# A conformer block on one core: another table of block order and of PSUM banks

## The chip, the core and the metric

The kernel runs on one core of a Trainium2 chip. The core has five engines that run their own instruction streams and meet through semaphores: TensorE (PE), whose weight loads (PEld) run beside its matmuls, VectorE (DVE), ScalarE (ACT), GpSimd (POOL) and SyncE (SP), which here issues the DMAs. PE writes its results to PSUM, of which the kernel uses banks 0 to 7; the other engines read them from there and keep everything else in SBUF. The metric is the device time of one execution in microseconds (us), as a median of several runs.

## The reference

One block of a speech model, for 2 sequences of 4000 tokens with 144 channels, in bf16: a feed-forward layer, self-attention with 4 heads of 36 channels, a gated convolution of 5 taps, another feed-forward layer, a last layernorm. The helpers (layernorm, softmax, silu, sigmoid) are the usual ones.

```python
def reference(x, w_ff1a, w_ff1b, w_qkv, w_o, w_pw1, dw, w_pw2, w_ff2a, w_ff2b):
    B, T, D = x.shape
    K = dw.shape[0]
    H = 4
    Dh = D // H
    h = _layernorm(x, axis=-1)
    h = _silu(h @ w_ff1a) @ w_ff1b
    x = x + 0.5 * h
    h = _layernorm(x, axis=-1)
    qkv = h @ w_qkv
    q = (lambda x, *d: x.transpose(*d))(qkv[..., :D].reshape(B, T, H, Dh), 0, 2, 1, 3)
    k = (lambda x, *d: x.transpose(*d))(qkv[..., D:2 * D].reshape(B, T, H, Dh), 0, 2, 1, 3)
    v = (lambda x, *d: x.transpose(*d))(qkv[..., 2 * D:].reshape(B, T, H, Dh), 0, 2, 1, 3)
    scale = Dh ** (-0.5)
    scores = jnp.einsum('bhqd,bhkd->bhqk', q, k) * scale
    p = _softmax(scores, axis=-1)
    att = jnp.einsum('bhqk,bhkd->bhqd', p, v)
    att = (lambda x, *d: x.transpose(*d))(att, 0, 2, 1, 3).reshape(B, T, D)
    x = x + att @ w_o
    h = _layernorm(x, axis=-1)
    h = h @ w_pw1
    a, b = (h[..., :D].copy(), h[..., D:].copy())
    h = a * _sigmoid(b)
    pad = K // 2
    hp = jnp.pad(h, ((0, 0), (pad, pad), (0, 0)))
    c = jnp.zeros_like(h)
    for i in range(K):
        c = c + hp[:, i:i + T, :] * dw[i][None, None, :]
    x = x + _silu(c) @ w_pw2
    h = _layernorm(x, axis=-1)
    h = _silu(h @ w_ff2a) @ w_ff2b
    x = x + 0.5 * h
    return _layernorm(x, axis=-1)
```

The costly part is the softmax attention: for each sequence and head there are 4000 x 4000 scores, 128 million in all, and each needs an exponential.

## The kernel before

**Tiles.** The 8000 tokens are 16 chunks (`CH` = 500), 8 for each sequence. Attention runs over chunks of queries; for each it walks the keys in tiles of 64 rows. One key tile and one chunk make a *tile of scores*: 64 keys by 500 queries for 4 heads, computed by a *quartet* of four 64x64 matmuls (`PS<-QT,KT`), each into half the partitions of one of two neighbouring PSUM banks. The exponential of a tile is a single ACT instruction over both banks, 128x1000 (`PT<-PS`), or, for some of the tiles, a few DVE instructions that build the exponential from the bits of a number (int16, then two uint16 operations and a product, also `PT<-PS` and `PT<-PT`). The result lies in one of 11 buffers of `PT`. A quartet of four matmuls of 64x37 (`PS<-PT,VA`, "PV" below) then sums values and weights into the two banks 6 and 7, which hold the output of the chunk until all its key tiles are through.

**Background.** Everything else goes on between these tiles: layernorms (`ST`, `RS`, `XN`, `AN`: statistics on DVE, the scaled rows on POOL or DVE), DMAs that turn rows into columns through a scratch tensor (`rows`, `XT`, `XTQ`), projections (`WQKV`, `WQ`), feed-forward tiles (`PS<-XT,WA` and `PS<-XT,WE`, then `TH`, a tanh on ACT, and `HT`, a product on DVE), residuals (`PS<-WB,HT` for a feed-forward layer, `PS<-WO,XT` after attention, `PS<-WP,SW` after the convolution; DVE adds them to `X`), the gate and the convolution (`PS<-XT,WP`, `U`, `PS<-U,DG`, `SW`), and small fillers on PE (`PS<-IDENT`). The front of the run is feed-forward and projections of the first sequence, until there are keys to attend to; the tail is the last chunk's convolution, second feed-forward layer and layernorm.

**How the order comes about.** The program is written as generators, one for each piece of background work, and a loop that plays the engines' clocks forward in a cost model. `Rec.op` records every operation with its dependencies, and each step of that loop makes one *block*: the operations of one step on one engine, such as the four matmuls of a quartet. On PE there are 2866 blocks, on ACT 1094, on DVE 1663, on POOL and SP some hundred each. When all 15,425 operations are recorded, `Rec.reorder` (line 263) puts the blocks of every engine into another order, read from the table `ORDER`: the character at place i of an engine's string says by how many places block i is moved (line 270):

```python
shift = [ALPHABET.index(c) - 45 for c in table[e]]
...
    at[i + shift[i]] = blk
```

`P` leaves a block at its place, `Q` moves it one place later, `O` one earlier. A second table, `PLACES`, gives one digit for each PSUM tile in the order in which tiles are taken: the first of its banks, 0 to 5 (`Rec.place`, line 241). After the move, `Rec.reorder` works out again which PSUM tile follows which in a bank, in the new order of PE, so that the first matmul of a tile waits for those that read the tile before it; it also sets which PV matmul of a sum starts it and which ends it. `Rec.finish` (line 323) turns the dependencies into semaphore waits, and `Rec.replay` (line 367) sends each engine its line of operations. Each engine runs its line strictly in order, so a waiting instruction holds up all behind it. All instructions are recorded under line 377, which is in `replay`; they are told apart by engine and tile names. The end of the kernel is

```python
R.reorder(ORDER)
R.finish(group_qs=("w0", "w1", "w2", "w3"))
```

Of the kernel before, what the change touches and what calls it, by code (L numbers as in the profile page):

```python
# [39 lines left out]
        "VOOROOBPPQOUPQMPRUQRTLQTQDPIPPQQQQQUQQHMRVOLRNNNPPPTOOOOPPPPQOROQRVOVPQMNPTROWQSLOUNOPXOUROMVMNZOS-R"  # L40
        "MKMOOOQOPQXQOLOOOOOXOOOPNOOOXOOOPNQNTMTOMNXNPNP_OLNQOLRNNN]OMRMOUKVMNYQMRPQHTYCMOLOWOMNNOROQLQOPTOOO"
        "ORROQLPVOOOOOUNOPPQQKPPPPPPPROSPRLTMTNNNOROOUORNORLORPQQSKO[_PYQRNOIFINLTLNNQNPSSNTMMYQNRRSMMSNUOCUP"
        "NYOVPROOJORRTNS>NNPTTOMNNUOOORNNTOOOOXROQSPPSQGXPPPPVOOOTROUSPPUQGPP3PPPQOPPPQRNOSOPXPPQOPVPQRPKBWSO"
        "OQNJOPZPNRNNNQQ]MQOQHPMSPPMKPPPPP^UOOPKMQRLQLRLNVPXMNNQMMTNNROMQQNURNOWRPMIQNNPPRRSNPKPPPPQQNPPPPPUP"
        "PPPQYIOOOOTNNOMRPRRVSPLXNSSMNTUOTJNTRMR8MPQSSOLQQTKQNNSPVMQMNOQNTQSMRNRJOUOOPNOQTNPSSLYLMRRMM]PNQIPM"
        "ORTMSOKQJSSSOSVJRPHPKPQOQOUPNOOQNPQRNOPPSOPNSOSQSQKRPRSOFRRMRMOSQSMRRKMRPNRUSMOTKMPTM_TRLMNQOPRSQMMW"
        "TOOOORO:VPNOOOOPQOPQOQOPROOPPPVOPQOWKPUOKOOVQOIOOOPPPPSOSOPRUQQHLXPPPQOVP_FLNNTMPNWZMPMGLMUMPNLOPQOP"
        "QOPQQURTNJOTROINSOOOQOTOOOQXMOOOPXMNNOOOOOPROOPPQOPPPPPPPPQOPPPPQSPUWQWIKPWJPJQVPQRKSNRfNPPQSSMNNb8R"
        "MMMRLMSMNQSLUN_ZOKNPN>TOLLMRLNQOSQOMPROURPNWO_HNNNNPPLOYNPRRKKPKSPMRN`RMQMMRSMMQNVVNVPXLNPRR@NSVO[NO"
        "OSNOVPMPNPTROSQSZROSQT(EOTJMOSQSNSJNSSPLULOO]NPMWNOOPKMNVMOOSNUMTLNNSMOTXMNNNOPNO]PNOTQNLMNOOORTQMMO"  # L50
        "PQRPSPPQUSGPTQQWQQUQTNCCMRPYPLOOSOOLRMOPPQ]QMNQOWOKNOMNRPRVJNRPMMQOURTMNLNSPSQLWROURPVZQTQTRW?ERAQGQ"
# [2019 lines left out]
```

## Time and profile before

| What | us |
|---|---|
| median of three runs | 887.04 |
| lowest and highest of them | 886.72, 887.05 |
| the profiled execution, a further one | 887.44 |
| its span, first to last instruction | 885.6 |
| wide exponentials on ACT, 128x1000 (806) | 749.1 busy, 1.075 each |
| feed-forward and gate activations on ACT (TH, 198) | 105.1 busy |
| scores on PE (3968 matmuls) | 425.6 busy |
| PV on PE (4712 matmuls) | 410.8 busy |

The granted clock of TensorE has a mean of 0.999 in the profiled execution, so the throttle plays no part. "Busy" is the time in which an engine had at least one instruction under way; a group's time is that of its own instructions. In the form `out<-in` the profile names the tiles that an instruction writes and reads with the buffers' numbers left out, and `[0.16 <-DVE HT L377]` behind an instruction says that the engine was idle for 0.16 us ahead of it and that the end of the wait came with DVE's write of `HT`. Lists of instructions in order of time give the start, the time from there to the end of the last of the group, and how many there were in a row. Matmuls of one row overlap: two quartets one behind the other start 0.21 us apart, though each is listed with 0.38.

DMA is idle for the most part (13.7% of 16 engines' span in the queue that carries nearly all of it), and POOL is busy for 303.9 us, a third of the span.

### The profile page before, as it was taken

The page shows a single profiled execution, that of the slowest core. Times are in us where ns is not written, and L with a number is a line of the kernel's source. Part 1 is how long each engine was busy: PE and PEld are TensorE (multiplying, and loading weights), DVE is VectorE, ACT ScalarE, POOL GpSimd, SP SyncE. Part 2 cuts the span into 40 slices and gives each one's busy share as a digit, 9 for nine tenths or more (in the row PEclk, how much of TensorE's full clock was granted, in tenths as well). Part 3 has the DMA queues.
Part 4 walks back from the last instruction along what each step waited for, and adds up shares of the span by engine and source line. Part 5 has one row for each costly group of instructions (what it writes and reads, how often), then busy time and mean ns, then how long its engine had stood idle before and what let it go on. Part 6 is the DMA issues. An engine that isn't in the chain of part 4 may idle for free.

```text
span 885.6 us, 27130 instructions
## 1 busy us (share of the span) xinstructions
PE 857.2 (97%) x11478; PEld 385.1 (43%) x11478; DVE 818.4 (92%) x1799; ACT 851.5 (96%) x1095; POOL 303.9 (34%) x584
## 2 busy tenths in 40 slices
PE   8999999999999999999999999999999999999996
PEld 7544333444444434344344444443434343444466
DVE  7968999999999999999988899997988999999987
ACT  6799999999999999999999999999999999999974
POOL 7761500216235235024107125241631017022733
PEclk9999999999999999999999999999999999999999
DMA  4231011112211111212101111002011001101101
GB/s 101 45 61 36 23 37 31 34 23 44 44 30 23 37 30 27 47 24 43 23 19 28 30 32 29 22 17 51 22 37 24 7 15 45 29 9 36 37 17 34
DMA packets 114222, 28.81 MB, mean 33 GB/s; under 512 B 101085, under 2 KB 114100, under 8 KB 114100
## 3 DMA queue, kind: packets, MB, share of 16 engines
q1 hardware_dynamic: 112642, 26.46, 13.7%
q8 instruction: 90, 1.47, 0.7%
q10 hardware_dynamic: 1458, 0.62, 0.3%
q14 instruction: 32, 0.26, 0.1%
HBM read 13.44 MB, written 13.61 MB: 31 GB/s over the span
## 4 chain that ended last, share of the span: by engine, by line
ACT 43%; PE 39%; DVE 14%; POOL 1%; DMA 1%; SPq 1%; issue 1%; DVEq 0%; POOLq 0%
ACT PT L377 39%; PE PS L377 39%; DVE PT L377 8%; ACT TH L377 4%; DVE ST L377 1%; DVE HT L377 1%; DVE X L377 1%; POOL XN L377 1%; DVE QT L377 1%; DVE XN L377 1%; DVE KT L377 1%; SPq L377 1%; DMA XTQ<-rows 1%; POOL RS L377 0%; DVE VA L377 0%
## 5 line engine op out<-in xcount | busy, mean ns | idle before, releaser
L377 ACT ACTIVATE PT<-PS 128x1000 bf16<-128x1000 f32 (+1 forms) x822 | 756.3, 1066 | 5.0 <-PE PS L377 3.8
L377 PE MATMUL PS<-QT,KT 64*64 64x500 bf16 x3968 | 425.6, 385 | 14.0 <-ACT PT L377 8.3
L377 PE MATMUL PS<-PT,VA 64*37 64x500 bf16 x4712 | 410.8, 372 | 2.0 <-DVE PT L377 0.7
L377 DVE TENSOR_SCALAR PT<-PS 128x500 int16<-128x500 f32 x372 | 244.6, 669 | 8.0 <-PE PS L377 6.5
L377 PEld LDWEIGHTS PS<-QT,KT 64*64 64x64 bf16 x3968 | 124.5, 104 | 240.3 <-ACT PT L377 135.5
L377 POOL TENSOR_SCALAR RS<-ST 125x4 f32<-125x4 f32 x130 | 35.2, 271 | 459.9 <-DVE ST L377 453.7
L377 PEld LDWEIGHTS PS<-PT,VA 64*37 64x37 bf16 x4712 | 141.2, 96 | 96.4 <-DVE PT L377 20.7
L377 POOL TENSOR_SCALAR XN<-X,RS 125x144 bf16<-125x144 bf16 x260 | 153.0, 622 | 8.0 <-DMA out_dram<-XN 1.3
L377 DVE TENSOR_SCALAR PT<-PT 128x1000 uint16<-128x1000 uint16 x372 | 150.6, 416 | 1.9 <-PE PS L377 0.5
L377 DVE TENSOR_TENSOR PT<-PT 128x1000 bf16<-128x1000 bf16 x186 | 126.5, 682 | 1.4
L377 ACT ACTIVATE TH<-PS 128x500 bf16<-128x500 f32 (+3 forms) x198 | 105.1, 554 | 4.0 <-PE PS L377 2.7
L377 POOL TENSOR_TENSOR RS<-RS,NHALF 125x4 f32<-125x4 f32 (+1 forms) x93 | 91.5, 987 | 36.2 <-DVE RS L377 30.4
L377 DVE SCALAR_TENSOR_TENSOR HT<-TH,PS 128x500 bf16<-128x500 bf16 (+1 forms) x135 | 80.8, 617 | 17.7 <-ACT TH L377 16.9
L377 PE MATMUL PS<-XT,WA 128*128 128x500 bf16 (+4 forms) x288 | 74.9, 365 | 0.4 <-DVE AN L377 0.2
L377 DVE BATCH_NORM_STATS2 ST<-X 125x6 f32<-125x288 bf16 x160 | 65.6, 446 | 3.1 <-DMA X<-in_x_dram 2.9
L377 DVE SCALAR_TENSOR_TENSOR X<-PS,X 125x288 bf16<-125x288 f32 (+1 forms) x128 | 57.2, 451 | 9.7 <-PE PS L377 8.6
L377 PE MATMUL PS<-WB,HT 128*125 128x144 bf16 (+1 forms) x640 | 51.9, 230 | 0.6 <-ACT HT L377 0.4
L377 PEld LDWEIGHTS PS<-WB,HT 128*125 128x125 bf16 (+1 forms) x640 | 44.2, 136 | 14.0 <-issue 4.6
L377 POOL COPY U<-U 128x2 bf16<-128x2 bf16 (+1 forms) x54 | 12.0, 260 | 71.4 <-DVE U L377 71.4
L377 PEld LDWEIGHTS PS<-XT,WA 128*128 128x128 bf16 (+1 forms) x288 | 21.2, 97 | 34.0 <-issue 12.5
L377 PE MATMUL PS<-U,DG 128*128 128x375 bf16 (+6 forms) x204 | 29.0, 264 | 0.2 <-DVE PT L377 0.2
L377 DVE STREAM_TRANSPOSE XN<-XN 128x320 f32<-128x320 f32 x54 | 27.0, 500 | 1.7 <-POOL XN L377 1.6
(93 smaller groups left out, 533.3 us busy)
## 6 DMA issues: line engine op xcount, KB each, us to landing
rows<-XN SPq DMA_DIRECT2D x216, 40.0 KB, 2.0
XT<-rows SPq DMA_DIRECT2D x56, 128.0 KB, 2.0
rows<-AN SPq DMA_DIRECT2D x60, 40.0 KB, 2.0
X<-in_x_dram SPq DMA_DIRECT2D x16, 140.6 KB
XTQ<-rows SPq DMA_DIRECT2D x26, 70.3 KB
out_dram<-XN SPq DMA_DIRECT2D x13, 140.6 KB
XT<-rows SPq DMA_DIRECT2D x56, 16.0 KB, 1.9
out_dram<-XN SPq DMA_DIRECT2D x3, 70.3 KB
```

What stands on the lines that cost most here:

```text
L377: ins = getattr(eng, o.name)(*o.a, **o.k)
```

## The change

Only the two tables change: five strings in `ORDER` and the digits of `PLACES`. In the strings, 1706 of PE's 2866 characters are different, 92 of ACT's 1094, 780 of DVE's 1663, 71 of POOL's 129 and 23 of SP's 154; 166 of 1720 digits in `PLACES`. The operations, their shapes, the buffers in SBUF and the code that reads the tables stay. With the new strings an operation may stand earlier or later on its own engine, a PSUM tile may lie in other banks, and the waits between the engines follow from that.

```diff
 ORDER = {
     "pe": (
-        "PPPPPPPPQOPPPRRRNLPPQSPROQQQHTOPPMRPRMQNV[NZMMMtMKPMOLIOOOQNQORRNTYLVESPPKLRPEEOOOQNPP[PNQNNQOMPP^PP"
-        "JPNPNQ[TLNKMQOKPNSQMNUOOOROSPPQXRGNPROUQYHKNNPNPNQQMPPPQOPWXNNNNPMM]]MNNOMQNLQLMMPPPTOOOOPPPQOUOOOOO"
-        "TWQWQKLJQNRPWITNNVOLLOORNOQOSYNNPMZNNNOMOOVN[PMSJPLQKQSQWQXHRWRVQRYWRHXR=BRALJRTMVOLWTLMPMPUUHOWORLO"
...
+        "PPPPPPPPQOPPPRRRNLPPSSOOLQQQMTOOPNQOPQQN|^N^MNNrJLNNNNHHLLMOOLQOQTWJVGRTNGHQSFFHMMOOPP]PNPNOQOMPPPQQ"
+        "JQOQOROVSOLNROLQQSPLOUOOOROSPPQXRGNYROUQIJKNNPUPNOPNPPPROOPVOOOOPNPUPNOOQNQOTQOPLPPPPPPPPPPPPPPPPPPP"
+        "TPQWQKPQQNRPFSUNOUOKPMOQ[NQNRXLMPL^LMMNRNNSMZOLTKOPNJPRPVPWIQVQUPQXVQQWQBCQ@KWQTLPYKTULINLOWTJOXORLN"
...
     ),
     "act": (
-        "PPPPPPPPPPPPQRSMNOPRPQQQKPPQOPQOPUOOOOOPPPRPQSQUNIVSSNORIIPPPPPPPPPPPPPQOPPQOPPPPPPPPQOPPPPPPPPPPPPP"
...
+        "PPPPPPPPPPPPQSSMNNSQNNQQNPPQOPQOPXOOOOOOOOPQQNSUOMTVTKLSKLMPPPPPPPPPPPPQOPPQOPPPPPPPPQOPPPPPPPPPPPPP"
...
     ),
     "dve": (
-        "PPQOQQQMPPQOaOOOOQR`MNJNOPLRNNYYHPMKOPJRNQJQQNRROQQQQIUPUPNSSSTGSSSTFSFRSSURUICZJSLOLPVOPNIXNNORNNPM"
...
+        "PPQOQQQMPPRPbMOOOQR`MNJNOPLQNNYYHOOLOPHRNQJQQNRROQQQQISSTOQ`RbSGGOPRIQIQSPRRUGEVTVEMKQVQRIIXMNORNNPM"
...
     ),
     "pool": (
-        "PQQQQSSOORPQTQOPQQTQQNQQQQQRRORPQQQQQ,PXOOOOOOO_NORNSMMNNOOQNNPWSNNOMPQQQKTTNNNNQQNPPPROTPMTOPTKNROQ"
...
+        "PQQQQRSOPRPQTQOPQQSQSNPQQQQQQSQOQQQQQ,PPPPPPPPPUOOOO]NROMNOVNNOMRMMPXOOPPMPPQQKUSNXMNLOOTNQSLPRJQRPQ"
...
     ),
     "sp": (
-        "PPPPPPPPQOPPPPPPPPPPPROQSMRNNPPPPPPPPPPPQOQOPPPPWOVNNNNNNPPPPPPRRNNRRNNPPPPPPPPRRNNPPZOOXNOMNNNNNVOO"
...
+        "PPPPPPPPQOPPPPPPPPPPPROQRMQNPPPPPPPPPPPPSOOQNPPPWOVNNNNNNPPPPPPRRNNRRNNPPPPPPPPRRNNPPZOOXNOMNNNNNSOO"
...
     ),
 }
 PLACES = (
-    "5024031421242530124140023035304230343105232504015043214352103245041522040241204124012401314032034023"
-    "2403240240340242043024034024032023403520430243024303420242034203402540524025405240524052404250524052"
...
+    "2341304015523150434105323035304230244135413412203025315242502403101510340241204124012401314032034023"
+    "2403240240340342042034024024032032404220430243024303420242034203402540524025405240524052404250524052"
...
 )
```

More of the change, by code (lines that the diff above doesn't have):

```diff
@@ L42 @@
[L42 to L51, printed above, removed]
@@ new lines @@
+        "OZPWQRHQKPLRWOS<OOPWJPNOOOOPPSOPNPPPPPSPPQQQQQHPQRRRRMQQQQQRTQNVRPQQ<QQHRPQQQKSOPTPQKQQSPPWQRSQLCUSJ"
+        "ORNKPQYQOLOPPMRRM[PQJQMTMPMMQQQQJZVOOPKMQULQKRLNWPXMNNPMMPNXQOMQOMYRNOPVINPMMVPPPPTOHOOPPPPPPPPPPWPP"
+        "PPPPYHOOOOTNNOMRPSQVTPLXNSSLNTUOTJNTRMR8MPQRYSLSQNLSHNVQLNQNNPRORNTNSPSTPVPRGGPRLORTTMYLNRSJN]KOQKPM"
+        "RNTMSOKVKUNTNSWLQQJFOOPPPPPSOOOQOPQVNPPPWOQOQOTRTRLSQSTPHSSNSNPRR3NSSPNSQOSVRNEULNQMN_SSNLMQOPRSQMMW"
+        "WOOOQOM=TPNOOQOPQOPXOOOPNOOOPPVOOOOPNPUOQOPVQOIOOOPPPPSOOOPRUQRMKYPPPPIPP[OKOOXNPNXZMMMGMNUMPNKOPUOO"
@@ new lines @@
+        "QOMSQTNXPJSPNOIO[OOOQNNOOOPXMOOOQOMOQOPPPQRNOPPPPPPRPNPPPQQNPPPPPTPY[QTJKP[IQJRLQQTKOORfOROQURLOMb6R"
+        "LMMRLNSMNQVLSNOYTKORN=TPKMRRMNROSNPNRRNUMPNVO[LNNNNPQMNWNVPQKNOJRPNROdRMQMMTTMNNNVQNVPVMNPTR?NSVOYNO"
+        "ORNOVPQQLPSXORPSYPNRPS(ENSMRNSPRORIORROSUKNNTNPMWNOOPSMNVMOOSNOMYSNNOMOPWMNUNOMNN_PNOOQNQMNOOOOSQMNP"
+        "PPPPVOPPSPKTUQOVPQUPROBERZOTPKOOKOOQQMPPRO^QMNRPSMKNRMNRPRVJNQQMMQOVTOMOMNSPSQLWROURPVZQTQTRS?ERAQGQ"
+        "QQ_PPPPPRFQRMKPPLYWNNPMOLNRROYSOZNFOLOXNOXNNGNNNOOeQNROOPUOPNWQMMBOMNSMPMRPNURNNSQNUPIQUMPLSOP]PJUNO"
@@ new lines @@
+        "MRNUKOOJQNPPYOORNNPQOWJOOOOPNSOOOPPPQOPPPPSPNUROOPQQTGOROTXKOMNPNRNNRXOMOPNOPNSTNN_MP_LNOQLYPKORIMMO"
+        "QUEOPPMQOPPTOPNURROMUPROOQSPTUQOLWOQ:NOOOPPPPPPPZTOP[QLPHTOPHKNOZOOOPNOOSORNKQOPPQQQZLOOOOOQOPLXOOOQ"
+        "NNOXNQNNOOPQWLOOOOOTNOOVNOOOOOTOOOTNOVNWPNWOPHWPISKPNWPZHQXNQVJQKFRRKQRWOEOPNPNPRORNOPWOQOQOPRROUFOO"
+        "OOP]OOOOOOOOOUOQNPQQQGP]OOOOOOQZNOSJMRLOLQRMRROLPPPSQUNPKSQTLPSOROSVOS_TN^[QNGIQOLLNNNW^1NNNNNPQOWJO"
+        "OLOPNPPQOPPZOORPNVOOINNRNOPVOPNQNTRLNVMOOOOO]OOOOOOOOOQNNPQ]NOOQRM]SKTVQITQWGGGROIdMOPQOLcVNLOPROSHJ"
@@ new lines @@
+        "NN[DNOMQMQOKOZRMVPLLNPNLPQOPPPUXOMYNLOLOMOOOPPPPQOSTPM[OKOO_NPQOSJNQHPQORRH[LOOOPNO[NNZMMNNXMOMN]IMN"
+        "NOOOOOWOMWMNYMMMQMMVOMNOOOUPNOOOPROOPPVOOXNOOLOOOOPXSOOQNPIOWOOOQNNOUSPURKKLUNOWPNLOOPQMQQNQRNOUQNPM"
+        "QQQLSQUSQSUMWPFFTOOKSVPNRXXNFKQWLLLMQUMRLNRPSSJNUROSJMNRTNVRcMTINRSNSFNOZFOOLOORWJZLLPULPKLOTLXUMMQL"
+        "MULTMNUMQUNOIORNOPPRRVNLOQORVKPMYPMPPRPVTGWJLMVLNNNPUMQOMTNPNOZOOORNNNOOOPPPPPPPPPTPSMOTPQJSPPKROOPS"
+        "OOOPPPPPPPPPQQRSQRRIVSSPSSKUCYQGRMQJYOOJXNNNNNNRNRMOPWOQZPMVNPPGPJQLPTROMNPPTPPPQTPXOGNOOOOQNPTRPMRP"
@@ new lines @@
+        "PPPQOPPPPPPPPPPPPPPPPPPPPPPPPPPPPPPPPPPPPPPPPPPPPPPPPPPPQOPPPPPPPPPPPPROORORNOQOPPPPPPPPPPPPPPPPPQOP"
+        "QQNPPQOPPPPPPPPPPPPPPPPPPPPPPPPPPQOPPQOPPPPPPPPPPPPROOPPPPPPPPPPPPPPPPPPQOPPPPPPPPPPPPPPPPPPPPPPPPPP"
+        "PQOQOPPPPPPPPQOPPPPPPPPPPPPPPPPPPPPPPQOPPPPPPPPPPPPPPPPPROQNPQQNPPPPPPPPPPPPPQOPPPPPPPPQOPPPPPPPPPPP"
+        "PPPPPPPPPPPPPPPPPSOOOPPPPPPPPPQOPPPPPPPPPPPPPPPPPPPQQNPPPPQOPPPPQQNPPQOPPQOPQOQOPPPPQOPPPPPPPPPPPPPP"
+        "PPPPPPPPPPQOPPPPPPPPPPPPPPPPPPPPPPPPPPQOPPROOPPPPPQOPPPPPPPPPPQOPPPPPPPPPPPPPPPPPPPPPPPPPPPPPQOPPPPP"
@@ new lines @@
+        "QOQOPPQOPPPQOPPPPPPPPPPPPPPPPPPPPPPPPPPPPPPPQQNPPPPPQOPPPPPPPPPPPPPPPPPPPPPPPPPPPPPPPPPPPPPPPPPPPPPP"
+        "PPPPPPPPPPPPPPPPPPPPPQOPPPPPPPPPQOPPPPPPPPQOQOQOPPPPPPPPPPPPPPPPPPPPPPPPPPPPPPPPPPPPQQQMPPPPPPPPPPPQ"
+        "OQOQOPPPPPPPPPPPPPPPPPPPPPPPPPPPPPPPPPPPPPPPPPPPPPPPPPPPPPPPPPQOPPPPPPPPPPQOPPPPPPPPPPPPPPPQOPPPQOPP"
+        "PPPPPPPPPPPQOPQOPPPQOPPPPPPPPPPPPPPPPPPPPPPPPPPPPQOPQOPPPPPPQOPPPPPPPPPPPPPPPPPPPPPPPPPPPPPPPPPPPPPP"
+        "PPPPPPPPPPPPPPPPQQNPPPPPPQOQOPPPPPPPROOQOQOPPPPQOPPQQQMPPPPROOSQNNQQQMRRSSPKKPPPPPPPQQQQLPPRPN"
@@ new lines @@
+        "PPQOPPQOROOQOQOQOPQOPcPNOOOOPQOQKNOOOOPNQORRSMVLNPNOOPPPPQSVPSQJRRIQSQSTPUUWPSG?JLOPPPPPUPUPPQSIPQSP"
+        "PQWQOQOPP=QOQOPROOSOSOPRKOPPPQQ_PLOOQNPPLO]NOOLOOPNOOSQMQLQOQOTRORNQJYOQOPPKPPMPPPQOPPTOTOOLOQQQQQSS"
+        "OSSPLRPBRPNPPPPPPPPPPQQRPQQQSHROQQQQQVQOEOTOMOQQSQRNQQRRORSBRMQXQRNRRMRURRORHRROQ;QQQRSOJSPRSQJQQQTP"
+        "SOOURBNNSNORNOROOQOPQOROOROOPPQOQOTPNPQUPKQNQMPPPSPNSPMOQSNOZQMQRNOQOPGPPPPQOPPPPPPXPNOOOPNOQOQOQQTQ"
+        "TPURTJPEQQIROOUQOQOQTPTOORDNQOQOPQQNQSPSLNOPPPPPPPQTPQRKRTQJSOROQQQQQSQSQMRPQSPUOP7P`PPPPPPPPPPCOOOO"
@@ new lines @@
+        "PRPNQOQOQOPPPPPPQOPPPPPPSOOSNOORORNRNQNPROOQOPPPPgOPNOOOPNOOOOOOQNNOOSNNNPPPPPPPPPQOROOPQOPRRNRPQKPP"
+        "PPROOPRPNQRNOQQNPQOQQNROOPPQOQRNQRMQNQQNQQNPPPQOPPPPPPPQQNPROOPQOQOPQUPPUOOPPQSQDNSOOOPPPPPSQORPRPRP"
+        "RPSDOQNPPQRPSPPQIQQNPPPPPPRRNNQQNQOPPQOPPPPPPQOPPPPPPPPPPPPPPPPRORPTLPUMUPLMNOPQQNPPQOPQOQOQOPPPPPPP"
+        "PPQQQQQKPSOOOQOPQOPQOPPTPPMOPPPROORPVPLOOOOPPPPPPPPPPQOPPRPNmPNOOOWNNNNNNNNOPNOPNPNQQMQORPIPQQRMRNOP"
+        "PPPPQOPPPPPPPPPPQOQOPQOQOPPPPPQOPPPPPPPPPPPPPPPPPPPPPPPSOPNPPPPPPPPPPPPSOOOPPPPQOPPPQQNRTNSMRMSLOOPQ"
@@ L98 @@
+        "OPQOYPRPRPJQRIQLPPPQOPPPPPPQOQOPRPNRPRPRPQIPSOORNOPQOQOSPN_ROLNQNUPLOLNPMSOOOQOPSSNSNLOPQOPPPPPQOPPP"
+        "QOPQOPPPPPPPPPQQQRPQQVPPPEOOPPPPPPQOQOPPPQTQSNKNPPPQRNOPQTQMRSLTOTJORLQQQKPSPRMNPPPQOPPPPPPPPPPPRSNP"
+        "RPKPPQQNPPPPPPROOSOOOPROOPPQRPQRROTQQSMROBPPPPROSNPSPPTRSSMRRKCRPQMPROQNPQOQOPPPSTOMPQRKOQOPQQQQRbQI"
+        "QOKOabQMMMNPNROTQQS@EGQQUPTQTCTW[NR^TTKCKBKLPPPKORSTNQXQQHPPQOF"
     ),
     "pool": (
-        "PQQQQSSOORPQTQOPQQTQQNQQQQQRRORPQQQQQ,PXOOOOOOO_NORNSMMNNOOQNNPWSNNOMPQQQKTTNNNNQQNPPPROTPMTOPTKNROQ"
@@ L106 @@
+        "OPZOOXNNNNNNNNTZNNNNOOOOVNNZNNNNOOOOOTNOPNPPPPPPPPPPQO"
     ),
@@ new lines @@
+    "3024203430243024024013402140204124024012042140204254052042502540425042504250542204303401340134013402"
+    "1402140234015310530153015302034204202430243203420342034302425042504240214205342034034014302430243024"
+    "3024032430243024302440254025402502052504524024023502352052405240524041204012412420140214021402140214"
+    "0214021402140214102141204021421431043103402141034204034014302535103502450425034204302403420342034203"
+    "5302430243024302430242040214034203413402045240524120425042540524052042021402014201421402140204240204"
@@ L127 @@
+    "1204120412041204102402424120412041214120401240214021402041204204523055203205240524052350235024302430"
+    "2430243034203420342034304024203240324024203350350230242420054311042401340242043203420420240124505240"
+    "2530523502325040254120423052350533203420423045240240250301542605436113451104506531532463145652501641"
+    "31401302321460502536"
 )
```

72 lines of the change are left out of this document (14 added, 58 removed).

## The prediction

> **What bounds the kernel now.** First the busy times, the chain of waits and the costliest groups on the page, then a table of busy time by stretch of the span.
>
> ```profile
> span 885.6 us, 27130 instructions
> PE 857.2 (97%) x11478; PEld 385.1 (43%) x11478; DVE 818.4 (92%) x1799; ACT 851.5 (96%) x1095; POOL 303.9 (34%) x584
> ACT 43%; PE 39%; DVE 14%; POOL 1%; DMA 1%; SPq 1%; issue 1%; DVEq 0%; POOLq 0%
> L377 ACT ACTIVATE PT<-PS 128x1000 bf16<-128x1000 f32 (+1 forms) x822 | 756.3, 1066 | 5.0 <-PE PS L377 3.8
> ```
> ```profile
> 0.00:40.00 40.00, 36.89 (x400) 25.77 (x401) 33.32 (x107) 28.53 (x56) 30.21 (x74) 1.00 0.34 79
> 40.00:80.00 40.00, 39.05 (x537) 17.35 (x537) 29.89 (x69) 38.56 (x53) 19.17 (x37) 1.00 0.23 52
> 80.00:800.00 720.00, 704.46 (x9554) 295.79 (x9555) 677.40 (x1417) 716.47 (x879) 217.82 (x410) 1.00 0.13 29
> 800.00:840.00 40.00, 38.97 (x542) 16.92 (x534) 39.78 (x88) 39.49 (x49) 20.39 (x38) 1.00 0.16 35
> 840.00:886.00 46.00, 37.81 (x466) 29.26 (x464) 38.02 (x122) 28.45 (x62) 16.34 (x28) 0.98 0.10 26
> ```
> The columns are PE, PE's weight loads, DVE, ACT and POOL. From 80 to 840 ACT is busy 716.47 + 39.49 = 755.96 of 760 us, idle 4.04, and the chain goes to and fro between ACT's exponentials and the matmuls that feed them. PE's 97% says less: its weight loads waited 148.4 us for ACT's PT in the table of waits, so PE is often full only because it is held up.
>
> Idle time hides part of ACT's waiting, because one activation can begin before the one ahead of it is done:
> ```profile
> 399.57 9.12 ACT L377 ACTIVATE PT<-PS 128x1000 bf16<-128x1000 f32 x10
> ```
> Ten in 9.12 us, of a shape whose mean is 1.07: less one for the last, nine spacings in 8.05, 0.89 each. Over the trace the 806 wide exponentials begin after each other by 0.884 in the shortest half, 0.900 at three quarters and 0.964 at nine tenths. What every ACT instruction takes beyond the fastest tenth of its own shape is waiting: 8.4 us in 0–40, 2.6 in 40–80, 21.1 in 80–840, 12.9 after that. No order can win more than this 45.0 from ACT's side. Of the middle's 21.1, 13.9 lie in 99 waits in which PE was still busy with other blocks when it should have begun the producer, 2.9 in gaps under 0.03, and some 4.3 in waits where PE itself waited for DVE or ACT.
>
> **The change part by part.** Every operation stays, with its shape: nothing is removed or added, so busy time keeps its sum, and only waits can change. Moved to another place on their engine are 7012 of PE's 11,478 instructions, 861 of DVE's 1799, 356 of POOL's 580, 57 of SP's 465 and 92 of ACT's 1103. So ACT runs nearly its old sequence, fed in another order. Changes between 64-square and full-array matmuls on PE go from 782 to 776, and waits on semaphores change by at most 10 on any engine (PE 1956 to 1963, DVE 1409 to 1419): I take both at nothing. The 57 moves on SP are loads and stores of background rows; the chain gives DMA and SP's queue 1% each, and ACT's middle waits name none of them: nothing.
>
> *Front (0–80).* PE sets it:
> ```profile
> 27.93 0.39 PE L377 MATMUL PS<-PT,VA 64*37 64x500 bf16 x4
> 28.25 0.63 PE L377 MATMUL PS<-XT,WA 128*128 128x500 bf16 x2
> 29.04 2.71 PE L377 MATMUL PS<-WB,HT 128*125 128x144 bf16 x40 [0.16 <-DVE HT L377]
> 31.68 0.41 PE L377 MATMUL PS<-QT,KT 64*64 64x500 bf16 x4
> ```
> ACT waits 2.64 us there for the scores that begin at 31.68, behind the 40 residual matmuls. In the new order one more feed-forward tile stands ahead of the residuals and the scores come later still, but the same ACT operations and almost the same PE work stand ahead of the exponential that begins at 44.70. What leaves the stretch ahead of its scores (44.16) is one PV quartet with its two changes of array form (27.93 to 28.25 = 0.32) and 4 of the 32 small projection matmuls (4/32 of about 0.64 = 0.08): −0.40. The bound above: the tile moved ahead of its operand stalls for one DVE HT (0.59) and one residual (0.68) is not hidden: +1.3. I take −0.40, because the work ahead is counted and the stall is not seen.
>
> *Tail (840–886).* PE sets it from 838 to 874 apart from a table load at 855:
> ```profile
> 858.78 0.84 PE L377 MATMUL PS<-WB,HT 128*125 128x144 bf16 x10 [0.25 <-ACT HT L377]
> 859.45 0.23 PE L377 MATMUL PS<-WP,SW 128*125 128x144 bf16 x1
> 859.52 0.23 PE L377 MATMUL PS<-WP2Z,SW 80*125 80x144 bf16 x1
> ```
> The four conv-projection matmuls from 859.45 (0.26) now stand ahead of the residual at 858.78 and fill its wait of 0.25: −0.25. In DVE's order two layernorm statistics (0.73 to 0.85 both) come ahead of the last chunk's, so its normalised rows come 0.65 later; that costs nothing while PE has its fillers and residuals from 860 to 870, and 0.35 to 0.65 if not. The other end, −0.75, is two more such waits filled. The last stretch from the final residual at 873.75 has the same order on DVE. I take −0.25.
>
> *Middle (80–840).* For each ACT instruction I took how its producer moved on PE against the ACT instruction ahead, weighing each matmul passed by its pace in the trace (a quartet of scores or PV 0.21, a feed-forward tile 0.44 to 0.46, a residual 0.62 to 0.68). Of the waits above 0.03, 125 with 18.3 us: 34 have less PE work ahead and give back up to 4.0; 67 with 10.3 us stay as they are; 24 with 3.8 us get more. One that gains:
> ```profile
> 100.84 1.15 PE L377 MATMUL PS<-PT,VA 64*37 64x500 bf16 x16
> 101.82 0.38 PE L377 MATMUL PS<-QT,KT 64*64 64x500 bf16 x4
> ```
> Four PV quartets run ahead of these scores and ACT is 0.25 late; the new order leaves three: −0.21. Among the activations that did not wait, 115 have producers moved behind by more than their slack; many are the same late place seen several times, and the distinct ones (some eleven, of 0.25 to 0.77) come to 5.2 us. One of these:
> ```profile
> 606.38 0.59 ACT L377 ACTIVATE TH<-PS 128x500 bf16<-128x500 f32 x1 [0.17 <-PE PS L377]
> ```
> A PV and a scores quartet now go ahead of its matmuls (about +0.53 with the change of form). So the ends for the middle are −4.0 and +5.2. The count of slack uses the old times, though, and a PE that has come ahead elsewhere meets such a place with more slack: PE has 760 − 743.43 = 16.6 us with nothing running in the middle and its weight loads wait 148.4 for ACT in all, so a late place of 0.5 is mostly made up ahead of it, while a wait that loses a quartet was bound by PE already and gains it all. The gains need less luck, but the next block binds behind each: I take half of them, −2.0, and nothing of the losses.
>
> Sum against the profiled execution of 887.44 (span 885.6 and 1.8 around it): −0.40 − 0.25 − 2.0 = −2.65, or 884.8. The median shown, 887.04, lies 0.40 below that execution: **884.4**.
>
> **The rivals.** A measurement of this kernel tells 0.2%, 1.8 us, from no change.
>
> *The middle gives nothing.* Each wait of which a quartet is taken is followed by another: PE's order is one line, and what leaves one gap is pushed into the next. For it: 10.3 of 18.3 us of waits keep their work ahead, PE runs 743.43 of 760 us, and gains and new lateness are near each other in sum (4.0 and 5.2). Against it: ACT's own sequence is nearly the same, so PE's slack can be shifted. Left are front and tail: 887.04 − 0.65 = 886.4, within 885.3 to 888.8. A page comes to the same end by another road: the Trainium skill (ScalarE: Activation LUTs, What ACT_TABLE_LOAD costs) gives an activation with immediate scale and bias 186 ns and 0.833 ns per element, 93 ns of it under the next one, an estimate of 0.926 us from one 1000-wide exponential to the next. By it ACT would hardly wait in the middle and no order could win there; the trace has half of them at 0.884, so it doesn't bear that out.
>
> *The late producers come through: slower.* The distinct late places, such as the feed-forward tiles near 295, 609, 788 and 828, stall ACT by all of the 5.2 while the gains hold at half: +5.2 − 2.0 − 0.65 = +2.55, or 889.6. It decides from the point where more than 2.65 of the 5.2 comes through (slower at all), 4.4 for more than 1.8 us slower. For it: in 800 to 840 ACT, DVE and PE are busy 39.49, 39.78 and 38.97 of 40, so nothing there can make up lost time, and DVE's own 861 moves were not weighed. Against it: the 148.4 us in which PE stood ready and waited for ACT.
>
> *The change doesn't do what it says.* If the new places only swapped blocks that wait for the same release, times would not move: 887.0. With 61% of PE's instructions elsewhere I give that no chance of its own; it lies within the first rival.
>
> **How the numbers follow.** Forecast 0.48, with its own range 881.5 to 885.2: all of the 4.0, −0.40 and −0.75 give 887.04 − 5.15 = 881.9, rounded down for gaps under 0.03 that close. No change 0.26. Slower 0.26, from 888.8; its price reaches 889.6, and past that only if the front's +1.3 or the loss of the gains comes on top (−0.25 + 5.2 − 2.0 + 1.3 gives 891.3). The range 881.5 to 890.0 leaves out about 0.05 below and 0.10 above. The chances: faster 0.48, same 0.26, slower 0.26.
>
> **What would show it.** Right: ACT's idle and excess spacing in 80–840 fall from 21.1 to about 19, the exponential now at 102.25 no longer waits, the one at 44.70 begins 0.4 earlier, PE's wait ahead of the residual at 858.78 is gone, and the number of each group is the same. Wrong: new ACT waits over 0.3 us behind feed-forward tiles near 295, 609, 788 or 828, DVE's HT or AN as releaser of PE more often than now, a gap ahead of the moved tile at 28, or a longer mean of a group, which a change of order alone should not bring.

## The result, and the profile after

The changed kernel takes 888.48 us (median of 22 runs, 887.22 to 894.07), the kernel before beside it 887.19 (22 runs, 886.72 to 887.85): a ratio of 1.0017 with a 95% interval of 1.0011 to 1.0023. It is slower by 1.29 us. That is less than the 0.2% named in the prediction, but the interval leaves no doubt of the sign, and the runs spread more than before.

The first lines of the page of the changed kernel, the same four as before (its profiled execution took 888.51 us):

```profile
span 886.7 us, 27139 instructions
PE 855.8 (97%) x11478; PEld 384.0 (43%) x11478; DVE 817.2 (92%) x1799; ACT 851.2 (96%) x1095; POOL 294.2 (33%) x584
ACT 52%; PE 29%; DVE 14%; DMA 2%; SPq 1%; POOL 1%; issue 1%; DVEq 0%
L377 ACT ACTIVATE PT<-PS 128x1000 bf16<-128x1000 f32 (+1 forms) x822 | 758.0, 1078 | 4.9 <-PE PS L377 3.6
```

The busy times hardly differ from those of before; only the shares of the chain move (ACT from 43 to 52%, PE from 39 to 29%). At a first look such totals don't show where 1 us in 887 went. Two other readings do. The first sets the start of the n-th ACT instruction of the new trace against that of the n-th of the old one. ACT's order is nearly the same in both, so the difference is how late the new kernel is at that place:

```
old time, us     62    76    91   102   127   230   309   577   674   777   848   872   span
lateness, us   0.04  0.69  0.64  2.22  2.81  2.28  2.1   1.90  1.49  2.24  1.62  1.71   1.1
```

2.2 us are lost between 91 and 127, then 1.3 are won back slowly until 674. Small losses stand at 70 and at 760, and the last 0.6 is won after the last matmuls. The second reading is the table of busy time by stretch, here with a stretch from 80 to 120 of its own, first of the kernel before and then of the changed one (the columns are as in the prediction: PE, weight loads, DVE, ACT, POOL):

```profile
80.00:120.00 40.00, 38.60 (x566) 14.75 (x567) 37.80 (x83) 39.82 (x45) 16.88 (x33) 1.00 0.14 29
```
```profile
80.00:120.00 40.00, 37.54 (x541) 14.58 (x543) 37.84 (x76) 37.58 (x43) 18.53 (x36) 1.00 0.12 26
```

ACT is busy for 2.24 us less there and PE for 1.06 less, but DVE is as busy as before with 7 instructions fewer. That points to a slow instruction on DVE. The instructions in order of time show which. First POOL and DVE of the changed kernel, then PE and ACT:

```profile
99.63 2.23 POOL L377 MEMSET AN<- 128x2560 bf16 x1
101.80 0.63 POOL L377 MEMSET U<- 128x640 bf16 x1
...
99.93 2.78 DVE L377 TENSOR_SCALAR PT<-PT 128x1000 uint16<-128x1000 uint16 x1
102.74 0.68 DVE L377 TENSOR_TENSOR PT<-PT 128x1000 bf16<-128x1000 bf16 x1
```
```profile
103.48 0.72 PE L377 MATMUL PS<-PT,VA 64*37 64x500 bf16 x8 [1.74 <-DVE PT L377]
104.03 0.38 PE L377 MATMUL PS<-QT,KT 64*64 64x500 bf16 x4
...
104.47 1.92 ACT L377 ACTIVATE PT<-PS 128x1000 bf16<-128x1000 f32 x2 [1.86 <-PE PS L377]
```

The 372 DVE instructions of that shape have a mean of 0.42 us. This one began 0.30 after POOL's memset of `AN` and ended 0.28 after the end of the memset of `U` behind it (101.80 + 0.63 = 102.43): it stood still while POOL wrote. The chain is then plain: PE's PV quartets wait 1.74 us for the `PT` that the product at 102.74 makes from it, the scores stand behind them in PE's order, and ACT waits 1.86 for the scores. In the kernel before, the same two memsets ran here:

```profile
58.90 2.24 POOL L377 MEMSET AN<- 128x2560 bf16 x1
61.07 0.64 POOL L377 MEMSET U<- 128x640 bf16 x1
...
59.42 0.68 DVE L377 CAST KT<-PS 128x500 bf16<-128x500 f32 x1 [0.61 <-PE PS L377]
60.02 0.50 DVE L377 STREAM_TRANSPOSE XN<-XN 128x320 f32<-128x320 f32 x1
60.44 0.64 DVE L377 CAST KT<-PS 128x500 bf16<-128x500 f32 x1
```

Beside them DVE had casts out of PSUM and a transpose, all at their usual lengths. So not every DVE instruction is held. What moved the memsets is one block of POOL's order: the one with both went from place 28 to place 32, behind four groups of layernorm scaling. Two of these wait for DVE's statistics (until 78.84 and 88.73 us), and the last ends where the memsets begin.

The trace of the kernel before already had a sign of it, beside POOL's layernorm scaling:

```profile
399.71 1.60 POOL L377 TENSOR_SCALAR XN<-X,RS 125x144 bf16<-125x144 bf16 x3
...
400.26 0.68 DVE L377 TENSOR_SCALAR PT<-PT 128x1000 uint16<-128x1000 uint16 x1
```

In that trace the 60 instructions of this shape that run beside such scalings alone take 0.450 us in the mean, the 232 with nothing on POOL beside them 0.408.

### The profile page after: what moved, and what is told of

Its sections match the earlier page's. It is cut to its first block, busy times and chain, and to the rows that moved or that the text cites. A ratio compares the mean times of both kernels' runs of the same rounds, so it can differ in the third digit from the quotient of the medians.

```text
span 886.7 us, 27139 instructions
## 1 busy us (share of the span) xinstructions
PE 855.8 (97%) x11478; PEld 384.0 (43%) x11478; DVE 817.2 (92%) x1799; ACT 851.2 (96%) x1095; POOL 294.2 (33%) x584
## 4 chain that ended last, share of the span: by engine, by line
ACT 52%; PE 29%; DVE 14%; DMA 2%; SPq 1%; POOL 1%; issue 1%; DVEq 0%
ACT PT L377 46%; PE PS L377 29%; DVE PT L377 7%; ACT TH L377 5%; DVE HT L377 2%; SPq L377 1%; DVE ST L377 1%; DVE X L377 1%; DVE XN L377 1%; DVE QT L377 1%; DMA rows<-XN 1%; DVE KT L377 1%; DMA XTQ<-rows 1%; POOL RS L377 1%; DMA X<-in_x_dram 0%
## 5 line engine op out<-in xcount | busy, mean ns | idle before, releaser
L377 DVE TENSOR_SCALAR PT<-PT 128x1000 uint16<-128x1000 uint16 x372 | 152.8, 422 | 1.7 <-PE PS L377 0.4
L377 POOL TENSOR_SCALAR XN<-X,RS 125x144 bf16<-125x144 bf16 x260 | 142.5, 580 | 9.0 <-DMA out_dram<-XN 2.4
L377 PE MATMUL PS<-U,DG 128*128 128x250 bf16 (+6 forms) x204 | 28.1, 264 | 0.0
```

What stands on the lines that cost most here:

```text
L377: ins = getattr(eng, o.name)(*o.a, **o.k)
```

## The experiments

All times are medians. Each kernel stands against runs of the kernel before on the same chip at the same time (887.03 for the first four, 887.24 for the next four, 887.35 for the last three). Kernels that take the order of one kernel up to a time and of the other from there on are cut where the blocks so far are the same set in both orders, on every engine: at 85 us after 194 blocks of PE, 110 of ACT, 139 of DVE, 30 of POOL and 17 of SP, at 835 us after 2750, 1024, 1553, 111 and 149. The banks follow the PSUM tiles.

### The memsets put back (e1)

One block in POOL's string, from place 32 to 28 (the four between move back by one):

```diff
     "pool": (
-        "PQQQQRSOPRPQTQOPQQSQSNPQQQQQQSQOQQQQQ,PPPPPPPPPUOOOO]NROMNOVNNOMRMMPXOOPPMPPQQKUSNXMNLOOTNQSLPRJQRPQ"
+        "PQQQQRSOPRPQTQOPQQSQSNPQQQQRRORPQQQQQ,PPPPPPPPPUOOOO]NROMNOVNNOMRMMPXOOPPMPPQQKUSNXMNLOOTNQSLPRJQRPQ"
...
```

> The changed kernel with one block put back: GpSimd's two memsets (AN 128x2560, U 128x640) go ahead of the four groups of layernorm scaling on POOL again, as before the change; all else as changed. Theory (the memsets, beside which a DVE instruction on PT from SBUF to SBUF took 2.78 us in place of 0.41, cost the time): that instruction takes 0.41 again, ACT's wait of 1.86 at 104.5 is gone, and the time falls by 2.0 to 2.4 from 888.5, to 886.1 to 886.5, under the 887.2 of before. Rival (the granted clock, 0.989 to 0.999 in the runs of the changed kernel, sets the difference): 888.5, with the same spread of clocks. Rival (the new order on DVE or PE sets it): 888.5, with ACT waiting in the same place.

885.64 (885.01 to 886.03): 2.84 under the changed kernel's median (2.68 when each is set against the kernel before beside it), and faster than before, with a ratio of 0.9983 (0.9975 to 0.9992). The DVE instruction in the profile, and ACT beside it:

```profile
100.11 0.41 DVE L377 TENSOR_SCALAR PT<-PT 128x1000 uint16<-128x1000 uint16 x1
...
99.79 7.34 ACT L377 ACTIVATE PT<-PS 128x1000 bf16<-128x1000 f32 x8
```

Eight exponentials run without a gap where the wait of 1.86 was. The gain is 0.4 to 0.8 larger than expected. The clock (below) went with the memsets; ACT's next wait did not: it is 0.46 at 110.44 in the changed kernel and still 0.37 at 107.49 here.

### The memsets moved late alone (e2)

The same block in the string of the kernel before, the other way:

```diff
     "pool": (
-        "PQQQQSSOORPQTQOPQQTQQNQQQQQRRORPQQQQQ,PXOOOOOOO_NORNSMMNNOOQNNPWSNNOMPQQQKTTNNNNQQNPPPROTPMTOPTKNROQ"
+        "PQQQQSSOORPQTQOPQQTQQNQQQQQQQSQOQQQQQ,PXOOOOOOO_NORNSMMNNOOQNNPWSNNOMPQQQKTTNNNNQQNPPPROTPMTOPTKNROQ"
...
```

> The kernel before with that one block moved alone: the two memsets behind the four groups of layernorm scaling on POOL, as in the changed kernel. Theory (the memsets): they run from about 101.9 to 104.7, DVE's uint16 instruction on PT that began at 102.32 and took 0.42 is held until 104.7, ACT waits some 1.5 to 2.0 more, and the time is 888.7 to 889.6 against 887.2. Rivals (clock, or the order on DVE or PE): 887.2.

889.66 (888.62 to 894.15), a ratio of 1.0039 (1.0025 to 1.0053): this one block costs 2.63 us in the old kernel too, just over what was expected. DVE and POOL of its profile:

```profile
102.27 2.52 DVE L377 TENSOR_SCALAR PT<-PT 128x1000 uint16<-128x1000 uint16 x1
...
101.72 2.22 POOL L377 MEMSET AN<- 128x2560 bf16 x1
103.89 0.62 POOL L377 MEMSET U<- 128x640 bf16 x1
```

The instruction named in the expectation (0.42 before) was held until 104.8, after the end of the second memset at 104.51. ACT waited 1.68.

### A shorter memset at the new place (e3)

```diff
-        op("pool", "memset", ANS[:, :, :], 0.0, w=[("AN", a) for a in range(NAN)], cost=2.2)
+        op("pool", "memset", ANS[:, 0:1, :], 0.0, w=[("AN", 0)], cost=2.2)
+        op("dve", "memset", ANS[:, 1:NAN, :], 0.0, w=[("AN", a) for a in range(1, NAN)], cost=0.0)
```

> The changed kernel with its order, but GpSimd clears a quarter of AN (128x640, some 0.63 us in place of 2.23) at the new place, and DVE clears the rest near 79 us, where it has room. Theory (the memsets hold the DVE instruction until they end): it takes 2.78 - 1.6 = 1.2 us, ACT's wait at 104.5 falls to 0.3 or less, and the time to 886.7 to 887.2. Rival (the place of the block on POOL matters because it holds up POOL's work behind it, not its length): 888.5.

886.32 (885.95 to 886.54), 2.16 under the changed kernel's median with POOL's order kept, and a little better than expected. The DVE instruction and the two memsets:

```profile
99.99 1.19 DVE L377 TENSOR_SCALAR PT<-PT 128x1000 uint16<-128x1000 uint16 x1
...
99.69 0.64 POOL L377 MEMSET AN<- 128x640 bf16 x1
100.27 0.64 POOL L377 MEMSET U<- 128x640 bf16 x1
```

POOL writes for 1.6 us less and DVE is held for 1.6 us less (1.19 against 2.78); ACT's wait falls to 0.27. The length of the writes is what counts, not the place of the block on POOL. (In this profile 0.6 us are lost between 76 and 83, where DVE now clears the rest: about what e3 stays over e1.)

### The parts of the change alone (e4 to e7)

e4 is the changed kernel with the memsets back and the old order up to 85 us. e5, e6 and e7 are the kernel before with the new order up to 85 us, from there to 835, and from 835 on; all have the memsets at the old place. The edits are long strings, each a splice of two orders at the cuts above.

```diff
 ORDER of e4, "pe", from the changed kernel:
-        "PPPPPPPPQOPPPRRRNLPPSSOOLQQQMTOOPNQOPQQN|^N^MNNrJLNNNNHHLLMOOLQOQTWJVGRTNGHQSFFHMMOOPP]PNPNOQOMPPPQQ"
+        "PPPPPPPPQOPPPRRRNLPPQSPROQQQHTOPPMRPRMQNV[NZMMMtMKPMOLIOOOQNQORRNTYLVESPPKLRPEEOOOQNPP[PNQNNQOMPP^PP"
...
```

> The changed kernel with the memsets put back and with the old order and banks of all engines up to about 85 us. Theory (the new front costs: at 83 us the changed kernel's ACT was 0.64 behind the old one's in the profiles): 0.6 less than with the memsets put back alone, 885.5 to 885.9. Rival (the front's lateness is made up later, or is noise of one profile): the same as that kernel, within 0.3.

884.66 (884.52 to 885.61), a ratio of 0.9974 (0.9966 to 0.9983) to before: with the new front out, the kernel is faster still, by 0.98 against e1.

> The kernel before, with the new order and banks up to about 85 us alone (the two memsets at their old place). The prediction's step for the front, -0.40: 886.6. Theory from the two kernels so far (memsets back 885.6, and with the old front too 884.7): the new front costs some 0.5 to 1.0 in the median, 887.5 to 888.0, because a feed-forward or K projection moved ahead meets its transposed rows (DMA XTQ<-rows) on the edge and waits 0.7 in some executions: a wider spread than before. Rival (nothing): 887.0.

887.22 against 887.24 (0.9989 to 1.0007): nothing either way.

> The kernel before, with the new order and banks from about 85 to 835 us alone (memsets at the old place). The prediction's step for the middle, -2.0: 885.0. Theory from the profile with the memsets back, in which ACT came 1.2 nearer between 90 and 840 us: 885.6 to 886.0, and in some executions 0.7 more where the feed-forward matmuls near 760 wait for DMA XT<-rows. Rival (the middle gives nothing): 887.0.

886.09, a gain of 1.15 (0.9979 to 0.9996), with a spread of 885.18 to 886.75: less than the prediction's 2.0.

> The kernel before, with the new order and banks from about 835 us on alone. The prediction's step for the tail, -0.25: 886.8. Theory from the sum (old front, new middle and tail 884.7, less 1.2 for the middle): -1.1, 885.9. Rival (nothing): 887.0.

886.60, a gain of 0.64 (0.9983 to 1.0001): the interval just takes in no change, and the gain is less than the 1.1 expected. The parts don't simply add: e6 and e7 make 1.79, e4, which has both, gains 2.37.

e5 missed the cost expected of it: the front alone is neutral, and yet e1, which has it, is 0.98 slower than e4, which has not. What in the front costs only together with the new middle was not found out. One candidate was seen, and it differs between executions: in the profile of the changed kernel PE waits at 70 us for transposed rows,

```profile
70.50 0.60 PE L377 MATMUL PS<-XTQ,WK 72*128 72x500 bf16 x2 [0.74 <-DMA XTQ<-rows]
```

while in the profile of e1, with the same order on PE, these matmuls begin at 69.45 with no wait listed. But this wait does not belong to the new front: in the kernel before the same matmuls wait 0.24, and in e6, with the old order there, 0.63. In the profiles of e1 and e4 ACT stands equally far at 83 us, 0.24 ahead of the kernel before. So the 0.98 stays open. A second place with a wait for rows that differs between executions lies in the middle, near 760.

### The place near 760 (e10)

e4 with the old order again from about 752 to 775 us (cut after 2455 and 2534 blocks of PE, 926 and 954 of ACT, 1387 and 1431 of DVE, 101 and 102 of POOL, 133 and 135 of SP).

> The changed kernel with the memsets put back, the old order and banks up to about 85 us, and the old ones again from about 752 to 775 us, where the feed-forward matmuls waited for DMA XT<-rows in some executions. Theory (that wait is what lifts some executions of the kernel with the old front, 884.5 to 885.6, by 0.7 to 1.0): median 884.3 to 884.7 and none over 885.2. Rival (the spread has another source): the same 884.7 with executions up to 885.6.

884.81, and no run over 885.03 (7 runs); e4 had three of ten from 885.18 to 885.61. The weight loads of the feed-forward matmuls, first in the profiled execution of e4 (885.45 us), then in that of e10:

```profile
758.72 0.57 PEld L377 LDWEIGHTS PS<-XT,WA 128*128 128x128 bf16 x4 [0.98 <-DMA XT<-rows]
```
```profile
758.80 0.57 PEld L377 LDWEIGHTS PS<-XT,WA 128*128 128x128 bf16 x4 [0.41 <-DMA XT<-rows]
```

No long execution was seen, as expected, but with three of ten before, seven without one can be chance (a probability of about 0.08); the median did not fall (884.66 and 884.81 can't be told apart). What the profiles show is the price: of the six with the new order here, ACT loses 0.6 to 0.8 us between 758 and 765 in three (the changed kernel, e4, e6) and nothing in the other three (e1, e3, e8); in e1's profile the loads list no wait for DMA at all. e10 loses nothing there.

### The end of the tail (e11, e12)

What the tail gains does not come before the last matmul: in the profile of e7 PE's last matmul begins 0.18 earlier than before, the same as at 835, but the span is 1.1 shorter. The order of the last three stores on ACT's queue is different. e11 is the kernel before with that alone:

```diff
     "act": (
...
-        "PPPPPPPPPPPPPPPPPQOPPPPPPQOQOPPPPPPPQOPQOQOPPPPQOPPQQQMPPPPTOOUQMMOUVMORSSMIJPPPPPQQQMPPPPPPQO"
+        "PPPPPPPPPPPPPPPPPQOPPPPPPQOQOPPPPPPPQOPQOQOPPPPQOPPQQQMPPPPTOOUQMMOUVMORSSMIJPPPPPQQQMPPPPPRPN"
     ),
```

> The kernel before with three blocks of ACT's order changed alone: the last three output stores that ACT issues go out in the order of the changed kernel (the store that waits longest last, in place of first). Theory (the tail's gain is the store that was stuck behind another one on ACT's queue): 886.4 to 886.7 against 887.1. Rival (the gain is the matmuls that fill PE's wait near 859, the prediction's -0.25): 887.1.

886.29 against 887.35 (0.9980 to 0.9998): a gain of 1.06, a little over the 0.4 to 0.7 expected. e12 is the complement: the new tail, with ACT's last three characters as in the kernel before.

> The kernel before with the new order and banks from about 835 us on, but ACT's three last stores in the old order. Theory (the stores are the tail's gain): 887.0 to 887.3. The prediction's step (waits filled on PE): 886.8. Rival (the gain lies on PE): 886.5.

887.68 against 887.35 (0.9996 to 1.0014): nothing won. The stores on ACT's queue, before and in e11:

```profile
880.70 1.22 ACTq L377 DMA_DIRECT2D out_dram<-XN  x3
```
```profile
876.84 0.29 ACTq L377 DMA_DIRECT2D out_dram<-XN  x1
...
879.81 0.72 ACTq L377 DMA_DIRECT2D out_dram<-XN  x2
```

In the kernel before, the store that waits for the last rows stood first, and two that were ready waited behind it: all three went out from 880.70, the last at 881.47. With that one put last, the first goes out at 876.84.

### Fillers in PE's gap (e8)

The runs of the changed kernel reach 894.07, and the long ones have a lower mean granted clock (0.989 in that one, under 0.997 in 12 of the 22, 0.999 at best). e2's runs are alike, down to 0.990 at 894.15. The kernel before (32 and more runs) and all kernels without the long memsets in the late place never fall under 0.997. So part of the price of the memsets comes with the clock: the eight runs of the changed kernel at 0.998 or more have a median of 887.84, 0.65 over the kernel before in place of 1.29, and the four such runs of e2 one of 889.02, 1.99 over it in place of 2.63. The table of busy time for the profiled execution of e2 (the clock is third from the end) shows where the clock falls:

```profile
104.40:107.81 3.41, 1.79 (x26) 0.60 (x26) 3.35 (x8) 1.73 (x3) 0.12 (x1) 1.00 0.00 0
107.81:111.22 3.41, 3.41 (x60) 1.67 (x52) 2.67 (x9) 2.73 (x3) 0.07 (x1) 0.50 0.02 5
```

PE is idle for 1.72 us from 104.29, and 1.8 us after it begins again TensorE has half its clock for 3.41 us; ACT then waits three more times (0.66, 0.23 and 0.27). The changed kernel's own profile shows no such stretch, but most of its runs have a clock that speaks for one. The Trainium skill (TensorE: Matmul & The Clock Gate, What's actually happening) has the clock halved after an idle window of about 3.4 us. The half and the length of the stretch agree; that a gap of 1.72 was enough in some executions does not. Nor does the place of the gap explain which execution is hit. In the clock's record of every profile taken here, the full clock lasts a whole multiple of 3.413 us (30 times and then 227 times in e2, 258 times in the changed kernel). In the stretch of that length ahead of e2's low clock PE was idle for 1.62 us (the first row above). In the changed kernel's profile one such stretch has 1.64 us of idle time, and no low clock follows:

```profile
99.97:103.38 3.41, 1.77 (x36) 0.72 (x28) 3.38 (x4) 2.63 (x3) 2.47 (x2) 1.00 0.17 47
```

To fill the gap, e8 puts matmuls of 12 columns into an unused corner of a bank, ahead of the waiting quartet:

```diff
+            if e == "pe":
+                k = next(i for i, o in enumerate(lines[e]) if o is self.ops0[1763])
+                lines[e][k:k] = self.extra
+                self.ops = self.ops + self.extra
...
+    for i in range(30):
...
+        o.k = dict(lhsT=IDENT[:, :], rhs=IDENT[:, 0:512 - CH], start=True, stop=True, skip_group_check=True)
```

> The changed kernel with 30 small filler matmuls put ahead of the PV quartet on PE that waits 1.74 us at 103.5 behind the held DVE instruction; the stall of DVE and ACT stays. Theory (a gap of 1.7 us on PE is followed, in some executions, by half the granted clock for some 4 us, as one profile shows at 108 to 111): no execution with a granted clock under 0.997, none over 889, median 887.4 to 888.0. Rival (the spread of the changed kernel has another cause): a median of 888.5 or more, and executions of 890 to 894 with clocks down to 0.99 as in the changed kernel.

889.22 (887.20 to 894.28), with clocks down to 0.989: the expectation failed. PE in its profile:

```profile
101.25 0.91 PE L381 MATMUL PS<-IDENT 128*128 128x12 bf16 x30
103.07 0.72 PE L381 MATMUL PS<-PT,VA 64*37 64x500 bf16 x8 [0.91 <-DVE PT L381]
```

The fillers lasted only 0.91 us and left 0.91 idle, and whether such narrow matmuls count for the clock no run shows. So the test doesn't tell. Shown is that the lower clock comes with the memsets in the late place (the changed kernel, e2, e8) and not without them; that it is PE's gap that does it was only argued.

## Why the prediction was wrong, step by step

*What bounds the kernel.* ACT's waiting does; this held. The lost time went through a wait of ACT for scores, and the gains came from such waits.

*"Every operation stays, with its shape: nothing is removed or added, so busy time keeps its sum, and only waits can change."* This is the step that failed. One DVE instruction went from 0.42 to 2.78 us because of what POOL did beside it. The text counted 356 moved instructions of POOL, and costed POOL's moves nowhere: it looked for what a moved instruction makes others wait for by semaphore, not for what it runs beside. e2 puts the price of that one block at +2.63 in the old kernel, e1 at +2.68 in the new one, against 0 in the sum. The last sentence of the prediction had named the sign of it, a longer mean of a group; on the page this is 416 to 422 ns for 372 instructions, first before and then after the change:

```profile
L377 DVE TENSOR_SCALAR PT<-PT 128x1000 uint16<-128x1000 uint16 x372 | 150.6, 416 | 1.9 <-PE PS L377 0.5
```
```profile
L377 DVE TENSOR_SCALAR PT<-PT 128x1000 uint16<-128x1000 uint16 x372 | 152.8, 422 | 1.7 <-PE PS L377 0.4
```

6 ns by 372 is the 2.2 us of a single instruction. The rows at 400 us above were a sign of it in the old trace. The rule for it was to be had: the Trainium skill (SBUF — State Buffer, Who interferes with whom) says that VectorE and GpSimd share one pair of ports as an exclusive lock, taken for a whole instruction by GpSimd or by a VectorE copy, cast or tensor_scalar in a mode that uses two ports, and that the other then blocks fully. The runs agree: the uint16 tensor_scalar within SBUF was held to the end of the memsets each time (2.78, 2.52 and 1.19 us in the changed kernel, e2 and e3), the casts out of PSUM beside the same memsets at 59 us were not.

*Front, -0.40.* Measured 0.0 alone (e5). The stall for DVE's `HT` ahead of the moved tile, which made the bound of +1.3, is there but small (0.27 in e5's profile). That the exponential at 44.70 begins earlier can't be told from the spread between executions: it lies from 0.49 earlier to 0.42 later in the five profiles with the new front, and 0.02 to 0.28 earlier in seven others with the old one. The transfers, costed at nothing, showed a wait of 0.74 in one profile and none in another, with the old order too (0.24, 0.63 in e6). In the company of the new middle the new front costs 0.98 (e1 against e4), which is left open.

*Middle, -2.0.* The direction was right, the size off: -1.15 alone (e6). Half of 4.0 was taken for the gains and nothing of the 5.2 for the losses; the second term is the mis-sized one. In e6's profile ACT comes 0.93 nearer between 83 and 835 us. The example of the prediction, the exponential at 102.25, came true: 0.24 won, 0.21 forecast. But 0.56 are lost right behind it, by 110, where ACT has a new wait of 0.37, and 0.79 near 760. Without these two the gains would be some 2.3. The loss behind 102.25 is in each profile with the new middle. Ahead of the scores that ACT waits for stand 32 small matmuls, first before, then in e6:

```profile
106.41 0.71 PE L377 MATMUL PS<-WQKV,XTQ 72*64 72x72 bf16 x32
```
```profile
106.50 1.05 PE L377 MATMUL PS<-WQKV,XTQ 72*64 72x72 bf16 x32
```

The same matmuls take longer in the new order; why, no run shows. The rival by which the middle gives nothing falls, and with it the estimate of 0.926 us for each exponential, from the Trainium skill (ScalarE: Activation LUTs, What ACT_TABLE_LOAD costs), by which no order could win there. The late places at 295, 609, 788 and 828 did not become the losses of the rival that ends slower: in e6's profile ACT loses 0.2 to 0.5 at single instructions near three of them, but comes out of all four stretches ahead of where it went in. That this rival's price, 889.6, lies near the 888.48 measured is chance. The largest single loss of the middle, near 760, was a wait for DMA, which the prediction had put at nothing because no middle wait of ACT named it. Now it names PE, and PE waits for the DMA: one step further back.

*Tail, -0.25.* Measured -0.64 (e7), but by another mechanism: filling the residual's wait is worth nothing (in e12's profile that wait of 0.25 is gone, but 0.33 now stand ahead of the four matmuls moved there), and the order of three stores on ACT's queue is worth -1.06 (e11). The text followed DVE's order to the end and missed that the DMAs that ACT issues are in ACT's order, too.

*The sum.* -2.65 was predicted. The parts alone make 0.0 - 1.15 - 0.64 + 2.63 = +0.84; the whole gave +1.29. Without the memsets' move the change gains 1.39 (e1), and without its front 2.37 (e4, 884.66): near the -2.65, but in part by luck, with less from the middle and front and more from the tail than forecast. The forecast of faster was lost on one block of POOL. e4 is, with e10, the best version measured here, under both kernels.

## What to carry to other kernels

When only the order changes, ask of every moved block not just who waits for it, but what it will run beside: here VectorE's uint16 instruction within SBUF stood still until GpSimd's memsets had ended, and 2.9 us of clearing buffers in the wrong place cost 2.6, as much as all the other moves could win (2.4 in e4). Put such clearing where VectorE reads PSUM, as at 59 us here, or ahead of the stage that counts. Look at the queue of every engine that issues DMAs, to its last entry: a store that waits first holds those behind it, and at the end of this kernel nothing hid that (1.06 us).

## What the runs showed of the hardware that was not expected

Two memsets of GpSimd, one behind the other, held the waiting VectorE instruction through both (102.43 and 104.51 were the ends of the second, 102.71 and 104.79 those of the held instruction): it did not slip in between. After a gap of 1.72 us on PE, TensorE's granted clock was 0.50 for 3.41 us in one profiled execution (e2), and not in another with a gap of 1.74 (the changed kernel), though a stretch of 3.41 us held 1.62 us of idle time in the one and 1.64 in the other.
